# A talking-heads attention with a dense layer on one core: scores two steps ahead, units placed by a table

## The chip, the core and the metric

The kernel runs on one core of a Trainium2 chip. The metric is the device time of the program in microseconds, the median of several executions; lower is better. The engines are named as the profile names them: PE (TensorE, with PEld for its weight loads), DVE (VectorE), ACT (ScalarE), POOL (GpSimd) and SP (SyncE, which here only issues transfers).

## The reference

Attention with two mixes over the heads, then a dense layer of two matrices with ELU between them. The shapes are q, k, v: 4 batches x 12 heads x 448 rows x 64; the weights of the dense layer 768 x 2048 and 2048 x 768.

```python
scores = scale * np.matmul(q, k.transpose(0, 1, 3, 2))
scores = np.einsum('bhij,hg->bgij', scores, w_pre)
scores = scores - np.max(scores, axis=-1, keepdims=True)
attn = np.exp(scores)
attn = attn / (np.sum(attn, axis=-1, keepdims=True) + 1e-09)
attn = np.einsum('bhij,hg->bgij', attn, w_post)
attn_out = np.matmul(attn, v)
...
x = attn_out.transpose(0, 2, 1, 3).reshape(B * S, H * D)
h = x @ w_in
g = np.where(h > 0.0, h, np.exp(np.minimum(h, 0.0)) - 1.0)
return g @ w_out
```

The dense weights come as 64-bit floating-point numbers and have to be turned into 32-bit ones on the chip.

## The kernel before

**Tiles.** A batch's 448 rows are cut into four blocks of 10, 12, 12 and 11 tiles of 10 rows (the last tile of a batch reaches past its end). A tile puts 10 rows x 12 heads on the partitions, so that both mixes over the heads are matrix products on PE. There are 16 blocks, and a *step* of the main loop handles two tiles of one block; a batch has 5 + 6 + 6 + 6 = 23 steps, and the whole loop N = 92. The last step of each batch has a single tile.

**Work of a step.** For two tiles, in the order of the data: `scores` multiplies the raw scores by the first mix (`s`, 8 matmuls, line 218, on two banks of PSUM, which one step fills), DVE takes the negated maximum (`nm`, line 223), ACT the exponential with its sum (`p`, line 225), `norm` the inverse of the sum on DVE (`rz`, lines 233 and 234) and on POOL the second mix scaled by it (`wz`, line 238), `post` the product of the two (`t`, 16 matmuls, line 247, two banks), and ACT copies the result (`at`, line 258).

**Units.** The raw scores of a block come from three *score units* of two head pairs each: `qk` (12 matmuls, line 191, in three terms of high and low parts, four banks), copies into `st` by DVE and ACT, and transfers `raw<-st` of 210 KB a head by SP (lines 204 and 207), which turn the layout into that of the tiles, in one of two buffers `raw0` and `raw1`, used in turn. The output of a block comes from three *output units*: `av` (32 matmuls, line 272, in the same four banks), a copy to `x` by DVE (line 284), and after the third a store of the block (`xd`). Ahead of a score unit q (and k, once in a batch) must be loaded from POOL's queue (lines 168, 156) and split into a high part on DVE (`qh` line 174, `kh` line 162) and a low part on POOL (`ql` line 175, `kl` line 163).

**Order.** Nothing is reordered by a scheduler: each engine runs its instructions in the order of the code, and waits on semaphores. In step `j` the loop issues `scores(j + LOOK)` with `LOOK = 1`, the score units and output units planned for `j`, `post(j)`, one or two steps of decoding, the planned loads and splits, and last `norm(j + LOOK)`. Where units stand is worked out from the first step of a block:

```python
at = [max(first[n - 1] + j, -LOOK) for j in (-2, 0, 2)]
```

and for output units `first[n] + length[n]` and 1, 3, 5 on. Loads of q stand four steps ahead of the first score unit, splits two.

**Decoding.** `Weights.run` is a generator; each `dec.step` runs it to its next `yield`. One of 48 pieces has a load `w<-in` (512 KB, POOL's queue, line 55), four operations of DVE on `c` (lines 69, 72, 78, 81), a square by ACT (line 76) and a store `s<-c` (256 KB, POOL's queue, line 85).

**Dense layer.** `Moe` reads x back from `xd` (`load_x`, line 417) and the decoded weights (`load_w`, line 402), splits both into high and low parts (`split_x`: ACT and DVE, lines 422 and 423; `split_w`: ACT and POOL, lines 409 and 410) and runs two halves of the rows: 16 products `h` (line 460) with the ELU, then 6 x 2 products `y` (line 528). The decoding goes on through the first half, eight steps ahead of each product `y`. Its beginning, `moe.begin`, stands in the attention's loop at step N - 7, where the buffers of the scores are given back, and `moe.ahead` splits the first x there.

Of the kernel before, what the change touches and what calls it, by code (L numbers as in the profile page):

```python
# [9 lines left out]
F32 = mybir.dt.float32  # L10
# [7 lines left out]
B, H, S, D = 4, 12, 448, 64  # L18
# [21 lines left out]
class Weights:  # L40
# [17 lines left out]
    def run(self):  # L58
        nc = self.nc
        self.load(0)  # L60
        yield
        for i, (_, dst) in enumerate(self.pairs):
            self.load(i + 1)
            w = self.w.pop(i)
            low, high = w[:, :, 0], w[:, :, 1]
            c = self.pool.tile([128, PW], I32, tag="c", name="c")
            sq = self.pool.tile([128, PW], F32, tag="sq", name="sq", bufs=1)

            nc.vector.tensor_scalar(
                c, high, 3, 0x3FFFFFF8, op0=ALU.logical_shift_left, op1=ALU.bitwise_and)  # L70
            yield
            nc.vector.scalar_tensor_tensor(
                c, high, -(1 << 30), c, op0=ALU.bitwise_and, op1=ALU.bitwise_or)


            nc.scalar.activation(sq, high.bitcast(F32), AF.Square)
            yield
            nc.vector.scalar_tensor_tensor(  # L78
                c, low, 29, c, op0=ALU.logical_shift_right, op1=ALU.bitwise_or)
            yield  # L80
            nc.vector.scalar_tensor_tensor(  # L81
                c.bitcast(F32), sq, 1.265625 * 2.0 ** -30, c.bitcast(F32),
                op0=ALU.is_ge, op1=ALU.mult)
            yield
            self.queue.dma_start(out=dst, in_=c.bitcast(F32))

    def step(self, n=1):
        for _ in range(n):
# [20 lines left out]
def attention(ctx, tc, qd, kd, vd, wpre, wpost, xd, dec, moe):  # L109
# [74 lines left out]
    def qk(n, hp):  # L184
        m = slots[n] * R
        (qh, ql), (kh, kl) = qs[n], ks[blocks[n][0], hp]
        got = [bank(ps_qk, "qk", 4) for hh in range(2)]
        for i, (q, k) in enumerate(((qh, kh), (qh, kl), (ql, kh))):
            for hh in range(2):
                part = slice(hh * 64, (hh + 1) * 64)  # L190
                nc.tensor.matmul(  # L191
                    got[hh][:m, :S], q[part, hp, :m], k[part], start=i == 0, stop=i == 2)
        return got

    def keep_qk(n, got):
        m = slots[n] * R
        for hh, copy in ((1, nc.vector.tensor_copy), (0, nc.scalar.copy)):
            for hp, ps in got:
                st = stp.tile([120, S], F32, tag="st", name="st")
                copy(st[:m], ps[hh][:m, :S])  # L200
                eng = nc.gpsimd if n == 0 and hh else nc.sync
                h, raw = 2 * hp + hh, raws[n % 2][:, :slots[n], :]
                if h < H - 1:
                    eng.dma_start(out=raw[h:h + 9 * GAP + 1:GAP], in_=st[:m])
                else:
                    for a, lo in enumerate((h, 64)):
                        eng.dma_start(out=raw[lo:lo + 4 * GAP + 1:GAP], in_=st[a * m // 2:(a + 1) * m // 2])

# [87 lines left out]
    for hp in range(0, NP, 2):  # L296
        eng = nc.sync if hp == 2 else nc.scalar
# [8 lines left out]
    for hp in range(NP + 1):  # L306
        if hp < NP:
            split_k(0, hp, nc.scalar.copy, nc.vector)
        if hp:
            keep_qk(0, [(hp - 1, qk(0, hp - 1))])  # L310
    nc.vector.tensor_scalar_mul(wa, wa, 1.0 / float(np.sqrt(D)))
    load_q(1, nc.gpsimd)
    split_q(1, nc.vector.tensor_copy, nc.gpsimd)

    LOOK = 1
    work, qks, avs = {}, {}, {}
    spare = ps_qk, "qk", 4

    def plan(j, f):
        work.setdefault(max(j, -LOOK), []).append(f)

    for n in range(1, NBL):
        b, i = blocks[n]
        at = [max(first[n - 1] + j, -LOOK) for j in (-2, 0, 2)]
        for u in range(3):
# [4 lines left out]
        if i == NB - 1 and b + 1 < B:  # L332
            for hp in range(NP):
                plan(at[hp // 2] - 2, lambda b=b + 1, hp=hp: load_k(b, hp, nc.gpsimd))
                plan(at[hp // 2] + hp % 2, lambda b=b + 1, hp=hp: split_k(
                    b, hp, nc.vector.tensor_copy, nc.gpsimd))
    for n in range(NBL):
        b, i = blocks[n]
        for u in range(3):
            j = first[n] + length[n] + (min(2 * u + 1, length[n + 1] - 1) if n + 1 < NBL else u)  # L340
            avs.setdefault(j, []).append((n, u))
# [6 lines left out]
    sc, nz = {}, {}  # L348
    for j in range(-LOOK, N + 3):
        if j == N - 7:  # L350
            op_ctx.close()
            spare = ps_t, "t", 2
            moe.begin()
        if j == N:
            moe.first()
        if 0 <= j + LOOK < N:
            sc[j + LOOK] = scores(*steps[j + LOOK])
        for n, u in qks.get(j, ()):
            keep_qk(n, [(hp, qk(n, hp)) for hp in (2 * u, 2 * u + 1)])
        for n, u in avs.get(j, ()):  # L360
            for w in range(2):
                av(n, 2 * u + w)
            keep_av(n, u)
        if j in nz:
            keep_post(*steps[j], post(nz.pop(j)))
        if LATE <= j < N:
            dec.step(1 + (j % 3 == 0))
        for f in work.get(j, ()):
            f()
        if j + LOOK in sc:  # L370
            nz[j + LOOK] = norm(*sc.pop(j + LOOK))
        if N - 5 <= j < N:
            moe.ahead(j - (N - 5))


class Moe:
# [57 lines left out]
        self.load_w(1)  # L434

    def ahead(self, step):
        if step < 4:
            for k in range(3):
                self.split_x(step // 2, step % 2 * 3 + k)
        if 1 <= step <= 2:  # L440
            self.split_w(step - 1)

    def first(self):
        self.h = [self.up(0, u) for u in range(2)]
# [142 lines left out]
```

## Time and profile before

| what | us |
|---|---|
| median of 3 executions | 990.58 |
| lowest, highest | 983.95, 992.04 |
| profiled execution | 986.33 |
| its span | 984.6 |
| first `s`, first `t` | 24.52, 31.39 |
| last `t` begins | 486.41 |
| first product of the dense layer | 487.25 |
| PE busy in the span | 896.1 (91%) |

The span is that of the profiled execution from its first to its last instruction; 1.7 us of that execution's time lie around it. Attention reaches from the start to 487 and the dense layer from there to the end. A row of a timeline gives the start, the duration, the engine and line, the operation, its output and inputs and how many instructions it joins; in brackets the idle time in front and what ended it. Groups by line give busy time, the mean of one in ns, and after the second bar the idle time of that engine in front of them, with what ended it.

### The profile page before, as it was taken

To read this page: it belongs to the slowest core of one execution; us is meant where nothing else is said; L and a number is where in the kernel's file an instruction comes from. 1 tells how busy PE (TensorE), PEld (TensorE's weight loads), DVE (VectorE), ACT (ScalarE), POOL (GpSimd) and SP (SyncE) were. 2 spreads that over 40 slices of the span, in tenths; PEclk is the share of its full clock that TensorE was granted. 3 is DMA by queue.
4 is the path that set the end of the run, shared out by engine and by line. 5 is a ranking of instruction groups with operands and counts; after the bars stand their busy time and mean duration, and the time that the engine had idled before them with its cause. 6 is when DMAs were issued, how large, how long until landed. Compare 5 with 4: busy or idle time off the path is not lost.

```text
span 984.6 us, 17943 instructions
## 1 busy us (share of the span) xinstructions
PE 896.1 (91%) x6576; PEld 738.8 (75%) x6576; DVE 515.9 (52%) x958; ACT 463.2 (47%) x988; POOL 440.4 (45%) x498
## 2 busy tenths in 40 slices
PE   3888998889878798999899999998899999999998
PEld 1556776657655576776688888887799999999997
DVE  5536765676545566665658888666602455510000
ACT  3545665556645466665635554323322555531111
POOL 2436545464334635433435555643342565543210
PEclk8979999999998999999999999999999999999999
DMA  5557556765565656858322222855532111212220
GB/s 177 164 155 208 181 177 199 224 179 165 172 172 180 182 154 190 247 154 228 112 67 93 81 81 85 226 200 179 190 118 68 59 55 49 75 53 93 81 73 29
DMA packets 79811, 137.20 MB, mean 139 GB/s; under 512 B 26100, under 2 KB 55576, under 8 KB 79724
## 3 DMA queue, kind: packets, MB, share of 16 engines
q1 hardware_dynamic: 63596, 81.14, 26.9%
q0 software_dynamic: 15584, 54.00, 17.9%
q8 instruction: 53, 0.87, 0.4%
q10 hardware_dynamic: 544, 0.92, 0.3%
q14 instruction: 34, 0.28, 0.1%
HBM read 72.84 MB, written 23.62 MB: 98 GB/s over the span
## 4 chain that ended last, share of the span: by engine, by line
PE 53%; DVE 14%; DMA 13%; issue 10%; POOL 7%; ACT 3%; POOLq 0%; SPq 0%; ACTq 0%; DVEq 0%
PE y L528 16%; PE h L460 13%; PE t L247 10%; PE s L218 6%; PE qk L272 4%; DMA raw<-st 4%; DMA w<-in 3%; PE qk L191 3%; DVE g L473 3%; DMA q<-in 3%; POOL wz L238 2%; DVE g L468 2%; DVE c L81 2%; DVE xl L423 2%; DVE c L78 2%
## 5 line engine op out<-in xcount | busy, mean ns | idle before, releaser
L247 PE MATMUL t<-wz,p 128*112 128x120 f32 x1440 | 180.2, 280 | 32.0 <-POOL wz L238 30.4
L247 PEld LDWEIGHTS t<-wz,p 128*112 128x112 f32 x1440 | 160.9, 183 | 59.6 <-POOL wz L238 43.1
L223 DVE TENSOR_REDUCE nm<-s 128x1 f32<-128x448 f32 x180 | 104.0, 618 | 134.2 <-PE s L218 134.2
L410 POOL TENSOR_TENSOR lo<-lo,hi 128x768 fp32r<-128x768 f32 (+1 forms) x56 | 117.6, 2100 | 123.8 <-ACT hi L409 123.6
L225 ACT ACTIVATE p<-s,nm 128x448 f32<-128x448 f32 x180 | 112.6, 630 | 124.9 <-DVE nm L223 124.9
L238 POOL TENSOR_SCALAR wz<-wb,rz 128x120 f32<-128x120 f32 x180 | 109.5, 617 | 111.9 <-DVE rz L234 97.5
L528 PE MATMUL y<-gh,lo 128*128 128x448 f32 x384 | 141.0, 367 | 10.1 <-POOL lo L410 10.1
L460 PE MATMUL h<-xh,lo 128*128 128x448 f32 x384 | 141.4, 368 | 5.6 <-POOL lo L410 5.5
L460 PE MATMUL h<-xh,hi 128*128 128x448 f32 x384 | 140.6, 366 | 0.3 <-ACT hi L409 0.3
L528 PE MATMUL y<-gh,hi 128*128 128x448 f32 x384 | 140.1, 365 | 0.3 <-ACT hi L409 0.3
L460 PE MATMUL h<-xl,hi 128*128 128x448 f32 x384 | 140.3, 365 | 0.0
L528 PE MATMUL y<-gl,hi 128*128 128x448 f32 x384 | 140.0, 365 | 0.0
L258 ACT COPY at<-t 112x480 f32<-112x480 f32 x180 | 98.3, 570 | 71.0 <-PE t L247 70.4
L479 POOL TENSOR_TENSOR gl<-g,gh 128x448 fp32r<-128x448 f32 x64 | 77.7, 1213 | 120.8 <-ACT gh L478 120.4
L218 PE MATMUL s<-raw,wa 64*64 64x448 f32 x720 | 99.2, 599 | 25.3 <-DMA raw<-st 22.8
L470 ACT ACTIVATE e<-g 128x448 f32<-128x448 f32 x64 | 37.1, 579 | 119.6 <-DVE g L468 119.6
L473 DVE SCALAR_TENSOR_TENSOR g<-e,g 128x448 f32<-128x448 f32 x64 | 55.5, 866 | 65.7 <-ACT g L471 65.7
L272 PEld LDWEIGHTS qk<-at,v 112*64 112x64 f32 x1312 | 64.1, 138 | 33.5 <-ACT at L258 21.9
L528 PEld LDWEIGHTS y<-gh,lo 128*128 128x128 f32 x384 | 72.4, 189 | 17.7 <-POOL lo L410 12.5
L460 PEld LDWEIGHTS h<-xh,lo 128*128 128x128 f32 x384 | 72.1, 188 | 15.0 <-POOL lo L410 9.4
L528 PEld LDWEIGHTS y<-gh,hi 128*128 128x128 f32 x384 | 72.4, 189 | 6.3 <-ACT hi L409 1.0
L460 PEld LDWEIGHTS h<-xh,hi 128*128 128x128 f32 x384 | 72.1, 188 | 6.5 <-ACT hi L409 0.7
(55 smaller groups left out, 1225.5 us busy)
## 6 DMA issues: line engine op xcount, KB each, us to landing
raw<-st SPq DMA_DIRECT2D x132, 210.0 KB
w<-in POOLq DMA_DIRECT2D x48, 512.0 KB, 5.6
lo<-s SPq DMA_DIRECT2D x80, 256.0 KB
s<-c POOLq DMA_DIRECT2D x48, 256.0 KB, 3.8
raw<-st SPq DMA_DIRECT2D x39, 175.0 KB
q<-in POOLq DMA_DIRECT2D x15, 360.0 KB, 6.6
v<-in POOLq DMA_DIRECT2D x24, 224.0 KB, 6.2
out<-o SPq DMA_DIRECT2D x24, 224.0 KB
```

Source lines behind the costliest of these rows:

```text
L218: nc.tensor.matmul(ps[a][w * 64:(w + 1) * 64, :S], wa[half], raws[n % 2][half, ts[0] + w, :], start=True, stop=True)
L223: nc.vector.tensor_reduce(nm, ps[i][:, :S], op=ALU.max, axis=AX.X, negate=True)
L225: nc.scalar.activation(p, ps[i][:, :S], AF.Exp, bias=nm, scale=1.0, accum_out=z[:, i:i + 1])
L238: nc.gpsimd.tensor_scalar_mul(wz, wb, rz[:, i:i + 1])
L247: nc.tensor.matmul(ps[:CJ, c * RH:(c + 1) * RH], p[:, c * CJ:(c + 1) * CJ], wz, start=True, stop=True,)
L258: nc.scalar.copy(ats[n][:, :, t, :], ps[:CJ, :NJ * RH].rearrange("p (c n) -> p c n", c=NJ))
L272: nc.tensor.matmul(ps[hh * 64:(hh + 1) * 64, w * m:(w + 1) * m].rearrange("p (t r) -> p t r", r=R), vs[blocks[n][0], hp][:, c, hh * 64:(hh ...
L410: self.nc.gpsimd.tensor_sub(lo_, f32(lo_), f32(hi_))
L460: self.nc.tensor.matmul(h, w[:, ks], x[:, k, :], start=n == 0, stop=n == 3 * NC - 1)
L473: nc.vector.scalar_tensor_tensor(g, e, 1.0, g, op0=ALU.add, op1=ALU.mult)
L479: self.nc.gpsimd.tensor_sub(self.gl[f][:, u, :], g, f32(self.gh[f][:, u, :]))
L528: nc.tensor.matmul(y[u], w[:, ks], g[f][:, u, :], start=f == 0 and n == 0, stop=f == NF - 1 and n == 2)
```

## The change

Scores are issued two steps ahead (`LOOK = 2`), and `norm` for the next step stands first in a step. Score units and output units stand at steps given by two tables relative to the start of a batch, and a unit's transfers are issued by `send`, one step later than its copies by `keep_qk`. Loads and splits of q and k stand further ahead of their unit. At the start the head pair 5 comes first, q of block 1 is loaded first of all, and block 1's first two score units come ahead of the loop. A decoded piece is stored one decode step later, after the next piece's load. The opening of the dense layer stands at N - 10 in place of N - 7 and its splits of x are spread over six steps, two in each, from N - 8; the late output units use the dense layer's banks from there.

```diff
@@ Weights.run
             yield
+            if i:
+                self.store()
             nc.vector.scalar_tensor_tensor(
                 c, high, -(1 << 30), c, op0=ALU.bitwise_and, op1=ALU.bitwise_or)
...
             yield
-            self.queue.dma_start(out=dst, in_=c.bitcast(F32))
+            self.done = dst, c
+        self.store()
@@ attention: keep_qk, send
+                out.append((2 * hp + hh, st))
+        return out
+
+    def send(n, out):
+        m = slots[n] * R
+        raw = raws[n % 2][:, :slots[n], :]
+        for h, st in out:
+            eng = nc.gpsimd if n < 2 and h % 2 else nc.sync
...
@@ the start
+    load_q(1, nc.gpsimd)
...
+    for hp, eng in ((4, nc.scalar), (2, nc.sync), (0, nc.scalar)):
...
+    order = 5, 4, 2, 3, 0, 1
+    for i in range(NP + 1):
+        if i < NP:
+            split_k(0, order[i], nc.scalar.copy, nc.vector)
+        if i:
+            hp = order[i - 1]
+            send(0, keep_qk(0, [(hp, qk(0, hp))]))
     nc.vector.tensor_scalar_mul(wa, wa, 1.0 / float(np.sqrt(D)))
-    load_q(1, nc.gpsimd)
-    split_q(1, nc.vector.tensor_copy, nc.gpsimd)
+    split_q(1, nc.scalar.copy, nc.gpsimd)
+    for u in range(2):
+        send(1, keep_qk(1, [(hp, qk(1, hp)) for hp in (2 * u, 2 * u + 1)]))
@@ the plan
-    LOOK = 1
+    LOOK = 2
+    RAW_AT = [(-10, -8, -6), (-4, -2, -1), (1, 3, 5), (7, 9, 11)]
+    OUT_AT = [(6, 8, 10), (12, 14, 16), (18, 20, 22), (23, 25, 27)]
...
-        at = [max(first[n - 1] + j, -LOOK) for j in (-2, 0, 2)]
+        at = [max(b * ROUND + j, -LOOK) for j in RAW_AT[i]]
...
-            plan(at[0] - 4, lambda n=n: load_q(n, nc.gpsimd))
+            plan(at[0] - 5, lambda n=n: load_q(n, nc.gpsimd))
...
-                plan(at[hp // 2] - 2, lambda b=b + 1, hp=hp: load_k(b, hp, nc.gpsimd))
-                plan(at[hp // 2] + hp % 2, lambda b=b + 1, hp=hp: split_k(
+                plan(at[hp // 2] - 5, lambda b=b, hp=hp: load_k(b, hp, nc.gpsimd))
+                plan(at[hp // 2] - 2 + hp % 2, lambda b=b, hp=hp: split_k(
@@ the loop
-        if j == N - 7:
+        if j == N - 10:
             op_ctx.close()
-            spare = ps_t, "t", 2
             moe.begin()
+            spare = moe.ps[0], "ps", 4
...
+        if j + LOOK - 1 in sc:
+            nz[j + LOOK - 1] = norm(*sc.pop(j + LOOK - 1))
         if 0 <= j + LOOK < N:
             sc[j + LOOK] = scores(*steps[j + LOOK])
-        for n, u in qks.get(j, ()):
-            keep_qk(n, [(hp, qk(n, hp)) for hp in (2 * u, 2 * u + 1)])
+        for n, out in ready:
+            send(n, out)
+        ready = [(n, keep_qk(n, [(hp, qk(n, hp)) for hp in (2 * u, 2 * u + 1)])) for n, u in qks.get(j, ())]
...
-        if j + LOOK in sc:
-            nz[j + LOOK] = norm(*sc.pop(j + LOOK))
-        if N - 5 <= j < N:
-            moe.ahead(j - (N - 5))
+        if N - 8 <= j < N:
+            moe.ahead(j - (N - 8))
```

**PE at the start of the loop.** The names are those of the program with a number for each buffer that is handed out: `s_417` and `s_418` are scores of step 2, `t_396` and `t_401` the second mix of step 0. Before:

```order
L191 MATMUL qk_376<-kh_225,ql_298 120x448
L191 MATMUL qk_377<-kh_225,ql_298 120x448
L247 MATMUL t_396<-wz_349,p_310 112x120 x4
L247 MATMUL t_401<-wz_351,p_314 112x120 x4
L218 MATMUL s_417<-raw0_168,wa_177 64x448
L218 MATMUL s_418<-raw0_168,wa_177 64x448
```

After, where `s_432` and `s_433` belong to step 2, `t_451` and `t_456` to step 0 and `s_472` and `s_473` to step 3:

```order
L233 MATMUL s_432<-raw0_168,wa_179 64x448
L233 MATMUL s_433<-raw0_168,wa_179 64x448
L262 MATMUL t_451<-wz_377,p_366 112x120 x4
L262 MATMUL t_456<-wz_379,p_370 112x120 x4
L233 MATMUL s_472<-raw0_168,wa_179 64x448
L233 MATMUL s_473<-raw0_168,wa_179 64x448
```

The second mix of step 0 stood ahead of the scores of step 2, and stands behind them now.

**POOL at the start.** Here `st` are the copies of block 0's scores, one a head, `q2` is the loaded q, and `ql` the low part of block 1's q; `raw0` is block 0's buffer and `raw1` block 1's. Before:

```order
L293 MEMSET raw1_169 128x2688
L204 DMA raw0_168<-st_201 10x10x448
L204 DMA raw0_168<-st_219 10x10x448
L204 DMA raw0_168<-st_237 10x10x448
L204 DMA raw0_168<-st_255 10x10x448
L204 DMA raw0_168<-st_273 10x10x448
L207 DMA raw0_168<-st_287 5x10x448 x2
L168 DMA q2_295<-in_0 128x720
L175 ISA
L175 TENSOR_TENSOR ql_298<-q2_295,qh_297 128x720
```

After:

```order
L176 DMA q2_171<-in_0 128x720
L309 MEMSET raw1_169 128x2688
L222 DMA raw0_168<-st_203 5x10x448 x2
L219 DMA raw0_168<-st_222 10x10x448
L219 DMA raw0_168<-st_240 10x10x448
L219 DMA raw0_168<-st_258 10x10x448
L219 DMA raw0_168<-st_276 10x10x448
L219 DMA raw0_168<-st_290 10x10x448
L183 ISA
L183 TENSOR_TENSOR ql_298<-q2_171,qh_297 128x720
L219 DMA raw1_169<-st_317 10x12x448
L219 DMA raw1_169<-st_319 10x12x448
```

The load of q moved from behind block 0's transfers to the head of the queue, the last head's two half transfers to the front of block 0's, and the first of block 1's transfers stand behind the low part.

**POOL in the first phase of `y`.** `lo` is the low part of a dense weight, `c` a decoded piece and `s2` its place in memory, `w` the next piece but one as loaded. Before:

```order
L410 TENSOR_TENSOR lo_7231<-lo_7231,hi_7230 128x1024
L85 DMA s2_10_107<-c_7265 128x512
L55 DMA w_7327<-in_6 128x1024
L85 DMA s2_11_108<-c_7329 128x512
L55 DMA w_7337<-in_6 128x1024
L410 TENSOR_TENSOR lo_7319<-lo_7319,hi_7318 128x1024
```

After:

```order
L435 TENSOR_TENSOR lo_7231<-lo_7231,hi_7230 128x1024
L55 DMA w_7326<-in_6 128x1024
L93 DMA s2_10_107<-c_7264 128x512
L55 DMA w_7336<-in_6 128x1024
L93 DMA s2_11_108<-c_7328 128x512
L435 TENSOR_TENSOR lo_7319<-lo_7319,hi_7318 128x1024
```

In each round the store stood ahead of the next load, and stands behind it now.

## Rows read from the trace of the kernel before

**Rows 1.** By stretch: us; PE, PEld, DVE, ACT, POOL busy; clock; DMA share; GB/s
```profile
24.50:487.50 463.00, 411.31 (x4141) 298.67 (x4142) 280.73 (x658) 275.23 (x671) 222.41 (x329) 0.96 0.61 181
400.00:420.00 20.00, 20.00 (x218) 14.74 (x216) 13.33 (x34) 13.28 (x32) 10.54 (x18) 1.00 0.85 260
618.20:748.80 130.60, 120.25 (x578) 108.61 (x577) 66.04 (x80) 36.35 (x58) 52.10 (x46) 0.99 0.56 176
```

**Rows 2.** Groups by line, PE from 31.39 to 487.5
```profile
L247 PE MATMUL t<-wz,p 128*112 128x120 f32 x1440 | 180.2, 280 | 32.0 <-POOL wz L238 30.4 <-DVE x L284 1.4
L218 PE MATMUL s<-raw,wa 64*64 64x448 f32 x704 | 96.2, 594 | 15.9 <-DMA raw<-st 13.4 <-issue 1.9 <-ACT p L225 0.5
L272 PE MATMUL qk<-at,v 112*64 112x120 f32 (+2 forms) x1312 | 72.9, 264 | 3.5 <-ACT st L200 3.5
```

**Rows 3.** Timeline of PE, 117.9 to 128
```profile
118.15 1.89 PE L247 MATMUL t<-wz,p 128*112 128x120 f32 x16
119.97 0.98 PE L218 MATMUL s<-raw,wa 64*64 64x448 f32 x8
120.88 1.86 PE L272 MATMUL qk<-at,v 112*64 112x120 f32 x32
122.67 1.89 PE L247 MATMUL t<-wz,p 128*112 128x120 f32 x16
124.50 0.98 PE L218 MATMUL s<-raw,wa 64*64 64x448 f32 x8
125.41 0.45 PE L191 MATMUL qk<-kh,qh 64*100 64x448 f32 x2
...
126.81 1.38 PE L247 MATMUL t<-wz,p 128*112 128x120 f32 x11
```

**Rows 4.** Timeline of PE, the start and the end of attention
```profile
24.52 1.77 PE L218 MATMUL s<-raw,wa 64*64 64x448 f32 x8 [9.38 <-DMA raw<-st]
...
31.39 1.90 PE L247 MATMUL t<-wz,p 128*112 128x120 f32 x16
...
486.41 1.07 PE L247 MATMUL t<-wz,p 128*112 128x120 f32 x8 [0.81 <-POOL wz L238]
```

**Rows 5.** Waits, 24.5 to 487.5: total us, times, longest us
```profile
DVE nm L223 <- PE s L218: 134.2, 82, 9.1
...
POOL s L85 <- DVE c L81: 67.9, 23, 5.7
...
PE t L247 <- POOL wz L238: 30.4, 26, 3.8
...
DVE qh L174 <- DMA q<-in: 14.6, 4, 8.7
```

**Rows 6.** Chain of waits, 262 to 310: start us, us, what
```profile
271.64 9.95 DMA raw<-st
...
293.16 10.24 DMA q<-in
```

**Rows 7.** Timeline of DVE, 210 to 217
```profile
211.30 3.60 DVE L233 TENSOR_SCALAR rz<-z 128x2 f32<-128x2 f32 x1
```

**Rows 8.** Timeline of POOL, 210 to 216.5
```profile
213.16 1.71 POOL L175 TENSOR_TENSOR ql<-q,qh 128x720 fp32r<-128x720 f32 x1
```

**Rows 9.** Timeline of DVE, 468 to 477.7, the end of attention
```profile
472.96 0.17 DVE L233 TENSOR_SCALAR rz<-z 128x2 f32<-128x2 f32 x1 [0.41 <-ACT p L225]
...
474.83 1.70 DVE L423 TENSOR_TENSOR xl<-xl,xh 128x448 fp32r<-128x448 f32 x3 [1.50 <-ACT xh L422]
```

**Rows 10.** The page, costliest groups: busy us, mean ns, idle before
```profile
L223 DVE TENSOR_REDUCE nm<-s 128x1 f32<-128x448 f32 x180 | 104.0, 618 | 134.2 <-PE s L218 134.2
...
L225 ACT ACTIVATE p<-s,nm 128x448 f32<-128x448 f32 x180 | 112.6, 630 | 124.9 <-DVE nm L223 124.9
```

**Rows 11.** Timeline of POOL, 648 to 667, the first phase of `y`
```profile
662.71 0.56 POOL L85 DMA_DIRECT2D s<-c  x1 [0.84 <-DVE c L81]
```

**Rows 12.** Waits, 618 to 748
```profile
PE y L528 <- POOL lo L410: 10.1, 7, 2.5
```

More of the change, by code (lines that the diff above doesn't have):

```diff
@@ L84, in run, with store @@
             yield
-            self.queue.dma_start(out=dst, in_=c.bitcast(F32))
+            self.done = dst, c
+        self.store()
+    def store(self):
+        dst, c = self.done
+        self.done = None
+        self.queue.dma_start(out=dst, in_=c.bitcast(F32))
     def step(self, n=1):
@@ L196, in keep_qk @@
         m = slots[n] * R
+        out = []
         for hh, copy in ((1, nc.vector.tensor_copy), (0, nc.scalar.copy)):
@@ L200, in keep_qk @@
                 copy(st[:m], ps[hh][:m, :S])
[L201 to L207, printed above, removed]
+                out.append((2 * hp + hh, st))
[5 more added lines that the diff above has]
+            eng = nc.gpsimd if n < 2 and h % 2 else nc.sync
+            if h < H - 1:
+                eng.dma_start(out=raw[h:h + 9 * GAP + 1:GAP], in_=st[:m])
+            else:
+                for a, lo in enumerate((h, 64)):
+                    eng.dma_start(out=raw[lo:lo + 4 * GAP + 1:GAP], in_=st[a * m // 2:(a + 1) * m // 2])
     def scores(n, ts):
@@ L295, in attention @@
     load_q(0, nc.sync)
-    for hp in range(0, NP, 2):
-        eng = nc.sync if hp == 2 else nc.scalar
+    for hp, eng in ((4, nc.scalar), (2, nc.sync), (0, nc.scalar)):
         eng.dma_start(out=k0[:, hp:hp + 2], in_=kd[0, hp:hp + 2].rearrange("h p s -> p h s"))
@@ L305, in attention @@
     split_q(0, nc.scalar.copy, nc.vector)
[L306 to L310, printed above, removed]
+    order = 5, 4, 2, 3, 0, 1
[5 more added lines that the diff above has]
+            send(0, keep_qk(0, [(hp, qk(0, hp))]))
     nc.vector.tensor_scalar_mul(wa, wa, 1.0 / float(np.sqrt(D)))
-    load_q(1, nc.gpsimd)
-    split_q(1, nc.vector.tensor_copy, nc.gpsimd)
-    LOOK = 1
+    split_q(1, nc.scalar.copy, nc.gpsimd)
+    for u in range(2):
+        send(1, keep_qk(1, [(hp, qk(1, hp)) for hp in (2 * u, 2 * u + 1)]))
+    LOOK = 2
     work, qks, avs = {}, {}, {}
@@ L322, in plan @@
         work.setdefault(max(j, -LOOK), []).append(f)
+    ROUND = sum(length)  // B
+    RAW_AT = [(-10, -8, -6), (-4, -2, -1), (1, 3, 5), (7, 9, 11)]
+    OUT_AT = [(6, 8, 10), (12, 14, 16), (18, 20, 22), (23, 25, 27)]
     for n in range(1, NBL):
         b, i = blocks[n]
-        at = [max(first[n - 1] + j, -LOOK) for j in (-2, 0, 2)]
-        for u in range(3):
+        at = [max(b * ROUND + j, -LOOK) for j in RAW_AT[i]]
+        for u in range(2 if n == 1 else 0, 3):
             qks.setdefault(at[u], []).append((n, u))
         if n > 1:
-            plan(at[0] - 4, lambda n=n: load_q(n, nc.gpsimd))
+            plan(at[0] - 5, lambda n=n: load_q(n, nc.gpsimd))
             plan(at[0] - 2, lambda n=n: split_q(n, nc.vector.tensor_copy, nc.gpsimd))
-        if i == NB - 1 and b + 1 < B:
+        if b and i == 0:
             for hp in range(NP):
-                plan(at[hp // 2] - 2, lambda b=b + 1, hp=hp: load_k(b, hp, nc.gpsimd))
-                plan(at[hp // 2] + hp % 2, lambda b=b + 1, hp=hp: split_k(
+                plan(at[hp // 2] - 5, lambda b=b, hp=hp: load_k(b, hp, nc.gpsimd))
+                plan(at[hp // 2] - 2 + hp % 2, lambda b=b, hp=hp: split_k(
                     b, hp, nc.vector.tensor_copy, nc.gpsimd))
@@ L338, in attention @@
         b, i = blocks[n]
-        for u in range(3):
-            j = first[n] + length[n] + (min(2 * u + 1, length[n + 1] - 1) if n + 1 < NBL else u)
-            avs.setdefault(j, []).append((n, u))
+        for u, j in enumerate(OUT_AT[i]):
+            j += b * ROUND
+            avs.setdefault(j if j < N else N + u, []).append((n, u))
             if i == NB - 1 and b + 1 < B:
@@ L346, in attention @@
         plan(hp + 1, lambda hp=hp: load_v(0, hp))
-    sc, nz = {}, {}
+    sc, nz, ready = {}, {}, []
     for j in range(-LOOK, N + 3):
-        if j == N - 7:
+        if j == N - 10:
             op_ctx.close()
-            spare = ps_t, "t", 2
             moe.begin()
+            spare = moe.ps[0], "ps", 4
         if j == N:
             moe.first()
+            spare = ps_t, "t", 2
+        if j + LOOK - 1 in sc:
+            nz[j + LOOK - 1] = norm(*sc.pop(j + LOOK - 1))
         if 0 <= j + LOOK < N:
             sc[j + LOOK] = scores(*steps[j + LOOK])
-        for n, u in qks.get(j, ()):
-            keep_qk(n, [(hp, qk(n, hp)) for hp in (2 * u, 2 * u + 1)])
+        for n, out in ready:
+            send(n, out)
+        ready = [(n, keep_qk(n, [(hp, qk(n, hp)) for hp in (2 * u, 2 * u + 1)])) for n, u in qks.get(j, ())]
         for n, u in avs.get(j, ()):
@@ L436, in ahead @@
     def ahead(self, step):
[L437 to L441, printed above, removed]
+        if step < 6:
+            for k in range(2):
+                self.split_x(step // 3, step % 3 * 2 + k)
+        else:
+            self.split_w(step - 6)
     def first(self):
```

## The prediction

> **What bounds the kernel now.** I began with the table of busy times by stretch. Attention, 24.5 to 487.5, is almost half of the span, and TensorE (PE) is busy 411.31 of its 463.00 us at a mean granted clock of 0.96; in 400 to 420 the same work runs without a gap, 20.00 of 20.00, at 1.00 [rows 1]. So PE bounds this stage, but not all the time: the reader is to see how much of the stage is loss, and which wait makes it. The groups by line say it. In front of `t` (the second mix) PE stands idle 32.0 us, 30.4 of it for POOL's `wz`; in front of `s` (the first mix) 15.9, 13.4 of it for the transfers `raw<-st`; in front of `qk` (the output product) 3.5 for ACT's copies of scores [rows 2]. That is 51.4 us. The rest of the loss is slower matmuls and small gaps, found by a pace: in a stretch without a wait the starts on PE's timeline lie 1.82 us apart from `t` to `s` (118.15, 119.97), 0.91 to the next unit, 1.79 over an output unit (120.88 to 122.67) and 1.40 over a score unit (125.41 to 126.81) [rows 3]. A step with no unit is thus 2.74 us, with an output unit 4.53, with a score unit 4.14. The loop has 91 steps behind the first, four of them with one tile in place of two (0.95 less each for three that count), 43 score units and 45 output units: 91 x 2.74 - 2.9 + 43 x 1.41 + 45 x 1.79 = 387.7 us. From the first `t` at 31.39 to the last at 486.41 it took 455.0 [rows 4]. **The loss is 67.3 us**: 51.4 in waits, and some 16 in matmuls slower than this pace.
>
> Why `t` waits for `wz`: the chain of a step is `s` on PE, `nm` on DVE, `p` on ACT, `rz` on DVE, `wz` on POOL, `t` on PE, and before the change PE has one step between `s` and `t` of a tile. DVE waits for `s` 82 times (134.2 us), so it is mostly early [rows 5]; but now and then something stands ahead of `rz` or `wz` in program order: DVE's `qh` waits 14.6 us in all for loads of q [rows 5], one of which took 10.24 us in the chain of waits [rows 6].
>
> **The change, part by part.** *Scores two steps ahead.* `t` of a step now stands behind the scores of two steps on, so between `s` and its `t` lies a whole step more, about 386/91 = 4.2 us. The longest wait of `t` for `wz` was 3.8 [rows 5]. The order of DVE's and POOL's own work around a cycle is the same, since `rz` and `wz` of a tile, moved to the head of a step, are the same operations between the same neighbours. So nearly all of 30.4 + 1.4 goes; I leave 2 (0 to 6, for waits that come in two steps running).
>
> What is late next is `s`. Two banks of PSUM hold both tiles of a step, so the next `s` can't begin before `p` has read them, and that loop has no more slack than before: from the end of `s` (119.97 + 0.98) to the next (124.50) are 3.55 us in a step with an output unit and about 3.16 with a score unit [rows 3], while `nm` (0.618) and two `p` (2 x 0.630) with their hand-overs need some 1.9 [rows 10]. The slack is 1.25 to 1.65. Anything that delays `nm` by more now costs directly. Two such things show. ACT and DVE together split the dense stage's x at the end of attention: three splits take DVE 1.70 us behind a wait of 1.50 for ACT [rows 9]. The change spreads them, two a step over six steps from the eighth last, which shortens each blockage to about 1.1 and 1.0; but the opening of the dense stage, three steps earlier, stands right behind the last score units, and the first x must land. I take 4 (0 to 9: the old blockage, 3.2 less 1.25 of slack in each of four steps, is 8). The other is `rz` at 211.30, held 3.60 us against 0.17 at 472.96, while POOL made a `ql` of 1.71 us with a `kl` ahead of it [rows 7 to 9]. With the change `ql` and a `kl` follow one another in one step of three batches, and `ql` still comes in every block: 3 us (0 to 8). Here the Trainium skill weighs against me: "SBUF — State Buffer", section "SBUF: two separate sides", says that VectorE and GpSimd share a pair of ports, as a lock that is kept for a whole instruction. The row agrees with it; by that rule every `ql` (12 x 0.4 beyond the slack) and the three pairs (3 x 1.6) would come through to `s`, 10 us in place of 3, and the forecast would be 7 later, 943, inside the range of my case.
>
> *The table of units.* A block's last score unit now always stands four steps before the block's first scores; before it was three, and two where the earlier block has five steps. Its transfers are put one step later into the program, so three steps, 12.7 us, remain for four issues of SP and a landing; the slowest in the chain took 9.95 [rows 6]. The 13.4 us before `s` therefore shrink: 3 left (0 to 6). Pace sets how much must move: 181 GB/s on average in attention; a 15% faster stage needs 210, and 400 to 420 carried 260 without stalling PE [rows 1]. One unit in nearly every step takes score and output units apart except in three steps, as before, so the 3.5 us in front of `qk` stay. Loads of q and k are issued two to three steps, not two, ahead of their splits: that is what is to keep `qh` from holding DVE. One score unit fewer is left in the loop (42): its stall-free sum is 386.3.
>
> *Clock.* PE's granted clock is 0.96 in the mean over attention, between its two levels of 1.2 and 2.4 GHz, and 1.00 where it had no gap; 4% of 411.31 us busy are 16 [rows 1], the same 16 that the pace leaves over. It is lost in stretches around the waits, so most goes with them; I leave 5 (0 to 8).
>
> *The start.* Block 0's first scores waited 9.38 us for their transfers, until 24.52; the first `t` came at 31.39 [rows 4]. The pair order and the earlier load of q for block 1 change little of the bytes; block 1's two units now run inside that wait, but send 8 x 210 KB on the same engines. If they ran ahead of block 0's last ones, 1.7 MB at 181 GB/s would cost 9 us; they are issued behind them, so I keep 31.4 (29 to 34).
>
> *Decode store a step later.* POOL no longer stands at the store for the last decode operation of the same step; in attention those waits (67.9 us in 23 places) held `wz` behind them [rows 5], which a step of lead covers anyway. In the first y phase it stood 0.84 us, and 0.56 for the store, before the next load could be issued [rows 11], and PE waited 10.1 us in 7 places for `lo` [rows 12], in a stretch with 130.60 - 120.25 = 10.4 idle [rows 1]. The load now goes ahead: 0.56 to 1.4 us in each of 7 rounds, 4 us less (0 to 9).
>
> **The sum.** What stays of stalls: 2 + 3 + 3.5 + 5 + 3 + 4 = 20.5 us (low ends 3.5, high ends 40.5). The last `t` ends at 31.4 + 386.3 + 20.5 + 1.1 = 439.3 in place of 487.5: 48.2 less. With the dense 4: 52.2. From the profiled execution's 986.33 that gives 934.1; its neighbours, 983.95 to 992.04, have a median 0.4% above it, and I take half of that: **936 us**. With all low ends 65.2 + 9 + 2.4 (start) go and 912 is left; with all high ends 28 - 2.6 and nothing in the dense stage, 963.
>
> **Rivals.** *The transfers take the wait's place.* If sends with a landing like 9.95 us queue behind loads that the faster pace brings closer together, `s` waits in each of 15 blocks for 2 us more (30), and the clock keeps falling after each (the 16 stay, 11 more than I left): 936 + 41 less some overlap, 958 to 977. For it: the share of the 16 engines is 0.61 on average and 0.85 where nothing stalls [rows 1]; against: that stretch.
> *The wait only changes its name.* If DVE's lateness and not POOL's order made `t` wait, `s` waits instead through its banks, for as long: 30.4 + 1.4 stay, and only the table and the decode store pay: 986 - 13 - 4 = 969 at best, 990 if the added score lead brings nothing. Against it: DVE waited for `s` in 82 of 92 steps, so it was seldom late itself [rows 5].
> *Slower: the loop `s`, `nm`, `p` becomes the bound.* If the moved `rz` is held regularly at the head of a step, with POOL on the shared data, `nm` is late in every step. At 2.5 us (between the 1.50 wait and the 3.60 of `rz` [rows 7, 9]) each step gives 2.5 - 1.25 away: 91 x 1.25 = 114 us, and attention ends at 31.4 + 386.3 + 114 + 5 = 536, 49 later: 1035. It decides from a mean lateness of 1.25 + 67/91 = 2.0 us. Against it: such a hold stands in this one row, and DVE was early enough to wait for `s` in 82 of 92 steps [rows 5].
>
> **Chances.** The forecast's case, 912 to 963, 0.70; transfers, 0.16; the changed name, 0.08, half of it within 1% (a measurement of this kernel tells about 1% from no change); slower, 0.03; better than 912, 0.03. Range 912 to 968, which takes in more than half of the transfers' case and leaves out about 2 in 10. Faster by over 1% 0.93, within it 0.04, slower 0.03.
>
> **What the changed profile would show.** Right: hardly any idle time in front of `t`, under 10 us in front of `s`, PE over 95% busy in attention at a clock of 0.98 or more, the first dense `h` near 439, some 6 us less idle at `lo` in the first y phase. Wrong: idle time in front of `s` put down to `p` or `nm` (the banks) or to `raw<-st`; a first `t` past 34; DVE idle before `qh`.

## The result and the profile after

The changed kernel takes **932.65 us** in the median of four executions (931.73 to 935.43), the kernel before 988.5 beside it; the ratio is 0.944 with an interval of 0.939 to 0.949. The forecast was 936. The profiled execution took 933.24 us with a span of 929.4, against 986.33 and 984.6.

The table by stretch for the kernel after (the columns are those of [rows 1]), attention and the first phase of `y`:

```profile
24.50:437.00 412.50, 395.99 (x4119) 289.19 (x4118) 275.58 (x654) 270.71 (x667) 222.75 (x331) 0.99 0.67 202
563.70:687.70 124.00, 117.75 (x577) 107.48 (x576) 63.90 (x78) 34.14 (x54) 48.50 (x45) 1.00 0.61 187
```

Attention is 50.5 us shorter than in [rows 1], PE is busy 96% of it in place of 89, the clock stands at 0.99 and not 0.96, and the transfers run at 202 GB/s. The groups by line of PE, in the window from the first `t`, show where the waits of [rows 2] have gone:

```profile
L262 PE MATMUL t<-wz,p 128*112 128x120 f32 x1440 | 171.1, 272 | 1.3 <-POOL wz L253 1.3
L233 PE MATMUL s<-raw,wa 64*64 64x448 f32 x699 | 93.2, 565 | 9.3 <-ACT p L240 9.3
L287 PE MATMUL qk<-at,v 112*64 112x120 f32 (+2 forms) x1280 | 71.4, 264 | 3.5 <-ACT st L209 3.5
```

In front of `t` 1.3 us are left of 32.0. In front of `s` no transfer ends a wait any more; its 9.3 us are now all for `p`, the release of the two banks. The 3.5 us at `qk` are the same to the tenth. The start and the end of attention on PE's timeline, beside [rows 4]:

```profile
24.58 1.77 PE L233 MATMUL s<-raw,wa 64*64 64x448 f32 x8
...
32.43 1.89 PE L262 MATMUL t<-wz,p 128*112 128x120 f32 x16
...
435.96 1.07 PE L262 MATMUL t<-wz,p 128*112 128x120 f32 x8
```

From the first `t` to the last are 403.5 us (455.0 before); the pace without a wait asked for 386.3, so 17.2 us of loss stay of 67.3. The largest piece of it lies in one place, the eighth step, which takes 10.31 us from `t` to `t` where 4.53 is the pace. PE, DVE and POOL around it:

```profile
63.82 1.89 PE L262 MATMUL t<-wz,p 128*112 128x120 f32 x16
69.69 1.64 PE L233 MATMUL s<-raw,wa 64*64 64x448 f32 x8 [3.98 <-ACT p L240]
```

```profile
67.59 0.43 DVE L69 TENSOR_SCALAR c<-w 128x512 int32<-128x512 int32 x1 [7.44 <-DMA w<-in]
67.93 0.16 DVE L248 TENSOR_SCALAR rz<-z 128x2 f32<-128x2 f32 x1
...
68.21 1.14 DVE L238 TENSOR_REDUCE nm<-s 128x1 f32<-128x448 f32 x2
```

```profile
60.21 1.14 POOL L55 DMA_DIRECT2D w<-in  x2
```

The first decoded piece is loaded and asked for in one step: POOL issues the load at 60.21, DVE stands at the first decode operation for 7.44 us, and `rz` and `nm`, which are behind it in the order of the code, are late. The lead of two steps saves `t` from this, but not the next `s`, which needs the banks.

The second piece is the first step of the loop, where DVE waits for q of block 2 and the next `s`, again, for `p`:

```profile
34.16 0.54 DVE L182 CAST qh<-q 128x720 fp32r<-128x720 f32 x1 [2.47 <-DMA q<-in]
```

```profile
36.31 2.38 PE L233 MATMUL s<-raw,wa 64*64 64x448 f32 x8 [1.99 <-ACT p L240]
```

This step takes 8.40 us; with its score unit it would take 4.14 at the pace. In the kernels below that leave the code up to there as it is, it takes from 6.18 (dec_early) to 11.13 (begin_old); 6.87 in control, the same program. A difference of attention that arises there can't be put down to their edits.

### The profile page after: what moved, and what is told of

The parts are those of the page before. It is cut to its first block, busy times and chain, and to the rows that moved or that the text cites. A ratio compares the mean times of both kernels' runs of the same rounds, so it can differ in the third digit from the quotient of the medians.

```text
span 929.4 us, 17904 instructions
## 1 busy us (share of the span) xinstructions
PE 889.5 (96%) x6576; PEld 733.6 (79%) x6576; DVE 497.3 (54%) x957; ACT 461.8 (50%) x989; POOL 445.4 (48%) x505
## 4 chain that ended last, share of the span: by engine, by line
PE 65%; issue 9%; DMA 8%; POOL 7%; DVE 6%; ACT 4%; SPq 0%; POOLq 0%; ACTq 0%; DVEq 0%
PE y L553 17%; PE t L262 14%; PE h L485 14%; PE s L233 7%; PE qk L287 7%; PE qk L199 6%; POOL gl L504 3%; DMA s<-c 2%; DMA raw<-st 2%; DMA w<-in 2%; POOL lo L435 1%; DVE xl L448 1%; DVE c L74 1%; DVE g L493 1%; DMA q<-in 1%
## 5 line engine op out<-in xcount | busy, mean ns | idle before, releaser
L253 POOL TENSOR_SCALAR wz<-wb,rz 128x120 f32<-128x120 f32 x180 | 113.8, 639 | 132.2 <-DVE rz L249 79.0
L262 PEld LDWEIGHTS t<-wz,p 128*112 128x112 f32 x1440 | 153.9, 177 | 25.5 <-issue 16.5
L262 PE MATMUL t<-wz,p 128*112 128x120 f32 x1440 | 171.1, 272 | 1.3 <-POOL wz L253 1.3
L485 PEld LDWEIGHTS h<-xl,hi 128*128 128x128 f32 x384 | 72.6, 189 | 6.6
```

What stands on the lines that cost most here:

```text
L253: nc.gpsimd.tensor_scalar_mul(wz, wb, rz[:, i:i + 1])
L262: nc.tensor.matmul(ps[:CJ, c * RH:(c + 1) * RH], p[:, c * CJ:(c + 1) * CJ], wz, start=True, stop=True,)
L485: self.nc.tensor.matmul(h, w[:, ks], x[:, k, :], start=n == 0, stop=n == 3 * NC - 1)
```

## The experiments

Each was measured beside the kernel before, and the ratio is to that. In the order of the table the first four share a chip, the next four another and the last four a third; where two kernels of different chips are compared, the ratios are the safer guide.

| kernel | median us | ratio to before | interval |
|---|---|---|---|
| look2_only | 1039.69 | 1.055 | 1.048 to 1.061 |
| look1 | 956.01 | 0.971 | 0.964 to 0.977 |
| store_old | 941.80 | 0.955 | 0.950 to 0.961 |
| better | 917.34 | 0.930 | 0.923 to 0.937 |
| control | 932.62 | 0.949 | 0.943 to 0.955 |
| look1_store_old | 972.81 | 0.989 | 0.984 to 0.995 |
| look1_loads_late | 964.15 | 0.980 | 0.973 to 0.986 |
| begin_old | 929.80 | 0.943 | 0.937 to 0.949 |
| start_old | 930.90 | 0.946 | 0.939 to 0.954 |
| dec_early | 914.65 | 0.931 | 0.925 to 0.937 |
| av_first | 926.26 | 0.941 | 0.934 to 0.948 |
| better2 | 911.66 | 0.926 | 0.919 to 0.933 |

**look2_only: the lead alone, in the kernel before.**

```diff
-    LOOK = 1
+    LOOK = 2
```

> The kernel before with LOOK = 2 and nothing else. Theory (the lead of two steps takes away the wait of t for wz, and the table is what gives the transfers the time that this costs them): t waits under 6 us in all in place of 31.8, but a block's last score unit now stands two steps, and one behind a block of five, ahead of its first scores, so s waits for raw<-st 40 to 70 us in place of 13.4; 990 to 1010 us. Rival 1 (the lead alone is the gain): raw waits stay near 13, 950 to 960 us. Rival 2 (the wait changes its name): s waits some 30 us for p, raw as before, 985 us.

It is slower by 5.5%. The waits of PE in attention, by total, times and longest:

```profile
PE s L218 <- DMA raw<-st: 65.5, 10, 11.3
PE s L218 <- issue: 15.5, 4, 6.1
PE s L218 <- ACT at L258: 4.7, 1, 4.7
PE s L218 <- ACT p L225: 2.7, 2, 1.7
```

No line for `wz` is left, so the lead takes that wait away by itself. But `s` waits 65.5 us for its transfers, five times the 13.4 of [rows 2]: taking the scores a step earlier took that step from the transfers. The time lies 30 us above the upper end of the theory. What the theory did not have: the clock fell too (0.91 in attention, 0.96 before), and 15.5 us of idle time in front of `s` have no releaser in the profile; what each of them costs was not separated.

**look1: the change without the lead.** The tables are shifted so that every distance to the scores stays.

```diff
-    LOOK = 2
+    LOOK = 1
-    RAW_AT = [(-10, -8, -6), (-4, -2, -1), (1, 3, 5), (7, 9, 11)]
-    OUT_AT = [(6, 8, 10), (12, 14, 16), (18, 20, 22), (23, 25, 27)]
+    RAW_AT = [(-9, -7, -5), (-3, -1, 0), (2, 4, 6), (8, 10, 12)]
+    OUT_AT = [(7, 9, 11), (13, 15, 17), (19, 21, 23), (24, 26, 28)]
...
-        if j == N - 10:
+        if j == N - 9:
```

> The changed kernel with LOOK = 1; the tables of score units and output units are shifted by one step together, so that every distance to the scores stays, and the dense layer opens one step later. Theory (the lead is what hides wz): t waits for wz 15 to 30 us again, raw waits stay under 3, the clock falls a little; 950 to 965 us. Rival (the table and the earlier loads already removed what made DVE and POOL late, the lead does little): t waits under 6 us, 931 to 938 us.

956.01, inside the theory's 950 to 965. In attention as a whole `t` waits nearly as long as before the change, and `s` for no transfer:

```profile
PE t L262 <- POOL wz L253: 29.4, 16, 6.4
PE qk L287 <- ACT st L209: 3.5, 3, 1.2
```

More than half of these 29.4 us lies at the end. The splits of x stand from step 84 on, behind 411 in this trace, and there `t` waits 16.6 us for `wz`, longest while DVE stands at the first split, with `rz` behind it; DVE, then PE:

```profile
417.17 1.16 DVE L448 TENSOR_TENSOR xl<-xl,xh 128x448 fp32r<-128x448 f32 x2 [5.45 <-ACT xh L447]
418.25 0.16 DVE L248 TENSOR_SCALAR rz<-z 128x2 f32<-128x2 f32 x1
```

```profile
419.45 3.54 PE L262 MATMUL t<-wz,p 128*112 128x120 f32 x16 [6.38 <-POOL wz L253]
```

Up to 411 it is 12.8 us, where the kernel before has 28.9 up to its own splits at 462. So the rest of the change takes away more than half of that wait in the loop without the lead; the lead takes the other half, and the waits at the end. By themselves the two parts are worth less than together: the change without the lead gives 3%, the lead without the rest costs 5.5%, both gain 5.6%. No run has the tables alone. With the old store (look1_store_old), the old start (start_old) or later loads (look1_loads_late) PE waits for no transfer either, so what brings the transfers in time is the tables and `send` together, which were not separated.

**store_old and look1_store_old: the decode store back in its place, with either lead.** Both kernels (after, and look1) are changed alike:

```diff
-            if i:
-                self.store()
...
-            self.done = dst, c
-        self.store()
+            self.queue.dma_start(out=dst, in_=c.bitcast(F32))
```

> The changed kernel with the decode store where it was, in the same decode step as its last operation and ahead of the next load but one. Theory (worth the load's lead in the first y phase alone): attention within 1 us, first y phase 3 to 6 us longer, 936 to 939 us. Rival (the store's wait on POOL also held wz in attention by more than the lead covers): attention 5 us or more longer with t waiting for wz, 941 or more.

> The kernel look1 (one step of lead, tables kept in their distances) with the decode store in its old place. In look1 t still waited 19.4 us for wz up to 430, 26.9 before. Theory A (the old store, at which POOL stood for DVE, held wz in attention): t waits 8 to 15 us more for wz, attention 8 to 15 longer, and the first y phase 4 to 7; 968 to 978 us. Rival B (the waits at the store lay in time that POOL had anyway; the table's distances and loads are the cure): attention within 3 us, only the y phase longer; 960 to 963 us.

With two steps of lead it costs 9 us by the medians (941.80 against 932.6; the intervals of the ratio overlap with control's), with one 16.8 (972.81 against 956.01). PE's waits in attention and the first phase of `y` in store_old:

```profile
PE s L230 <- ACT p L237: 12.4, 5, 4.5
```

```profile
574.40:705.30 130.90, 121.26 (x577) 110.06 (x576) 67.81 (x80) 36.39 (x58) 51.00 (x46) 0.97 0.56 175
```

The phase takes 130.9 us, nearly as in [rows 1], and 124.0 to 126.0 in after and control. Attention took 409.8 us from the first `t`, 404.3 in control. But 3.1 of these 5.5 us lie in the first step of the loop, ahead of any decoding, so they are not the store's. From step 8 to step 82 store_old is 3.2 us longer than control and 3.1 longer than after, and those two differ by 0.1: this is what the old store costs there. In one of the steps that lose, `rz` is held longer; after, then store_old:

```profile
291.02 1.72 DVE L248 TENSOR_SCALAR rz<-z 128x2 f32<-128x2 f32 x1
```

```profile
294.74 3.32 DVE L245 TENSOR_SCALAR rz<-z 128x2 f32<-128x2 f32 x1
```

In after POOL begins `ql` at 290.90, and `rz` ends with it; in store_old POOL, late from the store, begins `ql` at 295.19 and `kl` at 296.90, and `rz` ends with `kl`. At one step of lead attention is 8.8 us longer (13.5 in steps 8 to 82, less 3.0 behind them) and `t` waits 36.8 us for `wz` in place of 29.4. So the wait of POOL for DVE at the store did reach PE, and the second step of lead covers most of it, not all: 3.2 us are left of 13.5, by one trace each. The time of store_old's rival came true but not its sign, since `t` waits 1.3 us for `wz`, as in control.

**look1_loads_late: q and k loaded one step later, in look1.**

```diff
-            plan(at[0] - 5, lambda n=n: load_q(n, nc.gpsimd))
+            plan(at[0] - 4, lambda n=n: load_q(n, nc.gpsimd))
...
-                plan(at[hp // 2] - 5, lambda b=b, hp=hp: load_k(b, hp, nc.gpsimd))
+                plan(at[hp // 2] - 4, lambda b=b, hp=hp: load_k(b, hp, nc.gpsimd))
```

> The kernel look1 with the loads of q and k one step later, as far ahead of their splits as before the change (two steps in place of three). Theory B (the early loads cured DVE's late rz): qh waits for q 8 to 14 us again, t for wz 8 to 12 more, 964 to 970 us. Rival A (not the loads): qh waits under 5 us, 953 to 959 us.

The size is theory B's, 8.1 us more, but not its way. In attention up to 430 the wait of `qh` is

```profile
DVE qh L182 <- DMA q<-in: 2.3, 1, 2.3
```

as short as in look1 (2.2). What moved shows on POOL's timeline around one block's split, first in look1, then here:

```profile
193.60 1.82 POOL L183 TENSOR_TENSOR ql<-q,qh 128x720 fp32r<-128x720 f32 x1 [3.50 <-DVE qh L182]
195.38 1.13 POOL L171 TENSOR_TENSOR kl<-k,kh 128x448 fp32r<-128x448 f32 x1
196.49 1.98 POOL L253 TENSOR_SCALAR wz<-wb,rz 128x120 f32<-128x120 f32 x2
```

```profile
200.97 1.82 POOL L183 TENSOR_TENSOR ql<-q,qh 128x720 fp32r<-128x720 f32 x1 [3.49 <-DVE qh L182]
202.75 1.13 POOL L171 TENSOR_TENSOR kl<-k,kh 128x448 fp32r<-128x448 f32 x1
203.83 1.11 POOL L164 DMA_DIRECT2D k<-in  x2
204.97 1.51 POOL L253 TENSOR_SCALAR wz<-wb,rz 128x120 f32<-128x120 f32 x2
```

Issuing two loads of k, 1.11 us, came to stand between `kl` and `wz` in the very step that already holds both low parts, and `t` waited there (0.99 and 0.33 us in look1):

```profile
205.97 3.30 PE L262 MATMUL t<-wz,p 128*112 128x120 f32 x16 [2.47 <-POOL wz L253]
```

In attention as a whole `t` waits 36.5 us for `wz`, 7.1 more than in look1. Another 4 of the 8 us are the first decode operation: DVE stood at it for 6.7 us, 2.4 in look1; whether that comes from the moved loads was not tried.

**begin_old: the dense layer opened at N - 7, x split three at a time.**

```diff
-        if j == N - 10:
+        if j == N - 7:
...
-            spare = moe.ps[0], "ps", 4
+            spare = ps_t, "t", 2
...
-        if N - 8 <= j < N:
-            moe.ahead(j - (N - 8))
+        if N - 5 <= j < N:
+            moe.ahead(j - (N - 5))
```

and `ahead` itself as it was.

> The changed kernel with the dense layer opened at N - 7 and x split three at a time from N - 5, as before. Theory (a blockage of 3.2 us in four steps goes past the slack of the scores by two): steps 82 to 91 lose 8 to 12 us in place of 4.9, s waiting for p; 937 to 941 us. Rival (with two steps of lead the spreading is worth nothing): attention within 2 us, 930 to 935 us.

The rival held: 929.8, no difference to control, and the last ten steps of attention took 41.83 us from `t` to `t` in the trace, 41.69 in after and 41.73 in control (47.90 before, 58.63 in look1). Attention as a whole is 4.6 us longer than control's in this trace, but 4.9 of that lie in the first two steps of the loop, which the edit does not touch. With two steps of lead the spreading is worth nothing here.

**start_old: pairs in order, block 1's units in the loop.**

```diff
-            eng = nc.gpsimd if n < 2 and h % 2 else nc.sync
+            eng = nc.gpsimd if n == 0 and h % 2 else nc.sync
...
-    load_q(1, nc.gpsimd)
...
-    for hp, eng in ((4, nc.scalar), (2, nc.sync), (0, nc.scalar)):
+    for hp, eng in ((0, nc.scalar), (2, nc.sync), (4, nc.scalar)):
...
-    order = 5, 4, 2, 3, 0, 1
+    order = 0, 1, 2, 3, 4, 5
...
-    split_q(1, nc.scalar.copy, nc.gpsimd)
-    for u in range(2):
-        send(1, keep_qk(1, [(hp, qk(1, hp)) for hp in (2 * u, 2 * u + 1)]))
+    load_q(1, nc.gpsimd)
+    split_q(1, nc.vector.tensor_copy, nc.gpsimd)
...
-        for u in range(2 if n == 1 else 0, 3):
+        for u in range(3):
```

> The changed kernel with the old start: head pairs in their order, q of block 1 loaded behind block 0's transfers, and all three score units of block 1 in the loop. Theory (the start is bound by block 0's transfers, the rest hides): first t within 2 us of 32.4, block 1's two more units lie in steps -2 and behind, attention 0 to 4 us longer; 931 to 938 us. Rival (the early units and the pair order are worth their matmuls and the wait of block 0): first t 4 us later or more, and 938 to 945 us.

930.9, within its interval the same as control. The first `t` came at 34.87, 2.4 to 2.7 us later (the theory said within 2), and the loop's end 3.2 later in the profiled execution; so the start's new order is worth 3 us at most in a trace and is not to be told from nothing in the time.

**control, dec_early, av_first, better, better2: the changed kernel again, and what is left to gain.** dec_early loads the first piece ahead, by one `dec.step` more, which also puts every later decode operation one decode step earlier, in the dense layer too; av_first turns the two units around in the steps that hold both; better is both; better2 also loads q of block 2 ahead of block 1's transfers:

```diff
     split_q(1, nc.scalar.copy, nc.gpsimd)
+    load_q(2, nc.gpsimd)
...
-            plan(at[0] - 5, lambda n=n: load_q(n, nc.gpsimd))
+            if n > 2:
+                plan(at[0] - 5, lambda n=n: load_q(n, nc.gpsimd))
...
-        ready = [(n, keep_qk(n, [(hp, qk(n, hp)) for hp in (2 * u, 2 * u + 1)])) for n, u in qks.get(j, ())]
         for n, u in avs.get(j, ()):
             for w in range(2):
                 av(n, 2 * u + w)
             keep_av(n, u)
+        ready = [(n, keep_qk(n, [(hp, qk(n, hp)) for hp in (2 * u, 2 * u + 1)])) for n, u in qks.get(j, ())]
...
+        if j == LATE - 4:
+            dec.step()
         if LATE <= j < N:
```

> The changed kernel as it is, beside the three others. In its profile of before, a matmul of the dense layer started every 207 ns from 650 us on, against 200 to 203 in all other profiles of this study, which makes its last 270 us some 6 us longer. If that belongs to the kernel (its denser work), it shows again and the time is 930 to 936; if to one execution or chip, the pace is 200 to 203 and the profiled execution some 6 us shorter, 924 to 930 us.

> The changed kernel with the first load of a decoded piece issued four steps ahead of the other decode steps, and nothing else. Theory (at step 8 scores wait because DVE, in order, stands 7.4 us at the first decode operation): that wait goes, step 8 loses under 1 us in place of 6 to 7; 925 to 929 us, and the other 3.6 us of the kernel called better stay. Rival (the load only takes the transfers of v and q from their place): 930 to 934 us.

> The changed kernel with the output unit ahead of the score unit in the three steps that hold both, and nothing else. Theory: 3 x 1.2 us in front of qk go; 928 to 931 us. Rival (the score unit waits in its place for DVE's copy of the output unit's bank): 931 to 935 us, with as much idle time in front of the score units.

> The changed kernel with two edits: in the three steps that hold an output unit and a score unit the output unit stands first, and the first load of a decoded piece is issued four steps ahead of the other decode steps. Theory (the stalls left in attention are these): the 7.4 us of DVE at the first decode operation go, and with them 5 to 6 us of s; of the 3 x 1.2 us at the three steps most goes; 922 to 927 us. Rival (the bank of the output unit is needed by the score unit behind it, the wait moves to qk; the load only delays block 1's transfers): 930 to 934 us.

> The two edits of the kernel called better, and q of block 2 loaded ahead of block 1's transfers on POOL's queue. Theory: DVE's 2.4 us at qh in step 1 go and s waits 2 to 4 us less there; 913 to 918 us on the footing of 917 for better. Rival (the load takes the engines from block 0's or block 1's transfers at the start): first s or s of step 5 later, 917 to 922 us.

Control repeats the result (932.62). In dec_early DVE no longer waits for the first load, and the eighth step runs at the pace:

```profile
64.66 0.98 PE L233 MATMUL s<-raw,wa 64*64 64x448 f32 x8
67.10 1.90 PE L262 MATMUL t<-wz,p 128*112 128x120 f32 x16
68.92 0.98 PE L233 MATMUL s<-raw,wa 64*64 64x448 f32 x8
```

Its attention is 8.6 us shorter than control's, 395.7 to 404.3 from the first `t`. In av_first the line of `qk` waiting for `st` is gone from PE's waits (3.5 us) and no other has come in its place; attention is 399.9. In better2 these lines are all that PE waits for in attention:

```profile
PE s L233 <- ACT p L240: 3.5, 3, 1.9
PE s L233 <- DMA raw<-st: 0.5, 1, 0.5
PE qk L199 <- POOL kl L171: 0.3, 1, 0.3
```

better2, at 0.926 (0.919 to 0.933), is faster than both kernels of the case: 911.66 us. The four kernels came out below the ranges expected of them (dec_early 925 to 929, av_first 928 to 931, better 922 to 927, better2 913 to 918): the time fell further than the waits in attention say. dec_early gained 18 us, 8.6 of them there. In its profile the first half of the dense layer took 247.5 us (428.73 to 676.26), in control 256.7, in av_first, whose dense code and decode order are control's, 249.4. But in after, the same program as control, it took 250.9, so some 6 us in that half differ from one execution to another without any edit. What sets the waits there was not tried.

## Why the prediction was right, and where not

The waits that the change was to take away went, and for the reasons given. *The lead* removes the wait for `wz`: 2 us forecast, 1.3 measured; look1 brings 29.4 back, 12.8 of it ahead of the splits of x. *The table*, with `send`, removes the wait for transfers: 3 forecast, 0 measured; look2_only shows what the same transfers cost without the two, 65.5. The unit against unit stall stayed at 3.5 as said, and av_first shows its cause, the order of the two in the same banks. *The clock* rose to 0.99; one hundredth of 389.6 us busy is 4, with 5 forecast. The last `t` ended at 437.0 where 439.3 was forecast; the first `t` came at 32.43 for 31.4.

That the total came so close is in part luck. Two waits at the start of the loop, 5.8 and 4.3 us, were in no term. Against them stand terms that came out smaller (transfers by 3, `rz` by 1.5, `wz` and the clock by 0.7 and 1) and a pace that asked for too much: output units of blocks with fewer rows are shorter than its 1.79 us, some 4 us in all, and it counts a group of `s` for each of 91 steps, where two steps of lead and the steps of one tile leave 87 groups of eight matmuls behind the first `t`, 3.6 us less.

The rival of the transfers fell: PE never waited for one behind the first `t`, at a share of 0.66 and 202 GB/s. The changed name held for a small part: of 32 us in front of `t` some 9 now stand in front of `s`. The slower rival's mechanism is real but rare: of 92 `rz` in the trace after three were held 1.72 us (at 89.05, 190.19 and 291.02), each in a step that splits q and k together and until that step's `ql` ended; two of these steps lost 0.7 and 0.8 us, the third nothing. That agrees with the ports' lock in the Trainium skill ("SBUF — State Buffer", section "SBUF: two separate sides"). Its charge of 10 us was not paid: beside the other twelve `ql` no `rz` took over 0.33 us, and a hold of 1.72 stays close to the slack of `s`.

Three steps of the working were wrong in a part. First, that of the store: "in attention those waits held `wz` behind them, which a step of lead covers anyway". Even with the lead they cost 3.2 us of attention in steps 8 to 82, of 13.5 with one step of lead, so it covers three quarters; with 5 to 7 us in the first phase of `y`, 4 forecast, the edit is worth about 9 and not 4. By which wait the 3.2 us reach PE is shown for one step only.

Second, that the end would cost about 4 us was near (5.3 of the last ten steps' 41.69 are above the pace of 36.35, and 7.7 above one that leaves out the scores which the last two steps and half of the third last no longer issue), but the change's own spreading has no part in it. The lead shortens those steps, from 58.63 in look1; without the rest of the change it does not (48.21 in look2_only, 47.90 before).

Third, early loads "keep `qh` from holding DVE": at the same two steps of lead as before, `qh` waits 2.3 us and not the 14.6 of [rows 5], so the loads' lead is not what cured that wait. What the step's shift does is to move their issue out of POOL's way. The store that POOL used to stand at ahead of those loads is not the cure alone either: with it back and the earlier loads kept, in look1_store_old, `qh` waits 2.7. Whether the table is, or either of the two is enough, was not separated.

Not foreseen were the two waits at the start of the loop, the first decode load (5.8 us in step 8) and q of block 2 (4.3 in step 1, 2.7 in control); they now are the largest left, and go in dec_early and better2, where those steps take 4.26 and 4.84. In the dense layer the first phase of `y` took 6.6 us less, for 4 forecast, and 4.6 less in control; the wait for `lo` there, of which some 6 us were to go, fell from 10.1 to 6.3, and to 8.4 in control. In the profiled execution the second half gave 6.1 back by a slower pace, which control does not show.

## What to carry to other kernels

A step of lead for one chain is taken from another: before scores are issued earlier, count what their inputs have left, since the same line gained 2.5% with the tables (956 to 932) and cost 5.5% without. After such a lead look at the next loop that has none, here two banks that are freed only by the exponential, and price whatever stands ahead of it in the order of code, the first use of a freshly issued load above all. On a queue that both computes and issues transfers, each issue (0.55 to 0.60 us on POOL in the trace after) and each wait for another engine counts as work of the chain behind it.

## What was not expected of the hardware

In the profiled execution of after, a matmul of the dense layer's last 270 us started every 207 ns, in control every 200, both at a granted clock of 1.00 and with no idle time. The last phase of `y` on PE, after and then control:

```profile
849.95 0.37 PE L553 MATMUL y<-gl,hi 128*128 128x448 f32 x1
850.15 0.37 PE L553 MATMUL y<-gh,hi 128*128 128x448 f32 x1
850.36 0.37 PE L553 MATMUL y<-gh,lo 128*128 128x448 f32 x1
850.57 0.37 PE L553 MATMUL y<-gl,hi 128*128 128x448 f32 x1
```

```profile
849.98 0.36 PE L553 MATMUL y<-gh,hi 128*128 128x448 f32 x1
850.18 0.36 PE L553 MATMUL y<-gh,lo 128*128 128x448 f32 x1
850.38 0.36 PE L553 MATMUL y<-gl,hi 128*128 128x448 f32 x1
850.58 0.36 PE L553 MATMUL y<-gh,hi 128*128 128x448 f32 x1
```

The second half of the dense layer is 238.2 us long by it, and as long in begin_old's profiled execution; it is 232.1 in control and in all other profiles. av_first had the slower pace for a stretch: eight starts in a row lie 207 ns apart from 509.72 to 511.17, and 203 from 699.73 to 701.15. The same program shows both, so it is no property of the change; what sets it is open. Control's expectation had tied the time to it, 924 to 930 us at the faster pace, and that did not come: its profiled execution took 930.83, with the first half of the dense layer 5.8 us longer than in after. A comparison of two traces has to look at such stretches before it reads a difference of 6 us.
